# Attention with beacon keys, then a squared-ReLU MLP: last 128 output rows as two column halves, scores in 14 pieces per batch, attention released at four head pairs per MLP chunk

## The chip, the cores and the metric

The kernel runs on one core of one Trainium2 chip. The metric is the time of one execution on the device in microseconds (us); the kernel before takes 343.65 us, the median of 3 runs (343.54 to 343.87). Engines are named as in the profile: PE (matmul), PEld (the load of a matmul's stationary operand), ACT, DVE, POOL and SP. SP computes nothing here, it issues DMAs.

## The reference

All inputs and the output are float32. Attention has B=8 batches, H=8 heads, S=576 tokens and D=64, with Nb=16 beacon keys in front of each batch's keys that every token may see. The output of attention, laid out as 4608 tokens by 512, goes through an MLP whose middle is the square of a ReLU.

```python
k_all = np.concatenate([beacon_k, k], axis=2)           # 592 keys
v_all = np.concatenate([beacon_v, v], axis=2)
scores = scale * np.matmul(q, k_all.transpose(0, 1, 3, 2))
causal[:, Nb:] = np.triu(np.ones((S, S), dtype=bool), k=1)
scores = np.where(causal, -1000000000.0, scores)
a = np.exp(scores - scores.max(-1, keepdims=True))
a /= a.sum(-1, keepdims=True) + 1e-09
x = np.matmul(a, v_all).transpose(0, 2, 1, 3).reshape(B * S, H * D)
h = x @ w_in                                            # 512 -> 2048
out = np.square(np.maximum(h, 0.0)) @ w_out             # 2048 -> 512
```

## The kernel before

**Attention** goes by head pairs: 4 pairs per batch, 32 in all, numbered p. Keys of a batch are cut into 5 tiles c (four of 128 and one of 80). A score matmul (line 753) has a key tile as its stationary operand and a range of query columns t0 to t1 as its moving one; the two heads of a pair lie on the two halves of the PE's rows, so each entry of a piece is two matmuls. Only columns that the causal mask leaves are computed. A **piece** is what one exponential on ACT (line 768) takes: up to 512 columns in each of two neighbouring PSUM banks (one bank per head), written as bf16 into the tile `pt`. The list `WHOLE` (line 681) cuts a pair into 4 pieces of 496, 464, 416 and 288 columns, 1664 in all, from 6 key-tile ranges, so 12 matmuls. Batch 0 uses another list, `SPLIT`. Then come the mask on DVE (lines 783 and 787), 30 matmuls of probabilities by values (line 803, with a column of ones that gives the sums), and the division on DVE (lines 818 and 819) into `xn`. For batches 1 to 7 a DMA transpose (line 850, five per batch, issued by SP) brings `xn` to `xT`, which the MLP reads.

**The MLP** goes by 9 chunks of 512 tokens: 64 matmuls of 512 columns with w_in (line 931), ReLU on ACT or DVE (lines 948 and 950), the square on DVE (line 957), 64 matmuls of 512 columns with w_out (line 968: 4 blocks of 128 tokens, 16 matmuls each), an ACT copy of each block into `osb` (line 437), and a store to `out` (line 991; for the last 256 rows one store per block, line 993). Chunk j needs tokens 512j to 512j+511; so chunks 3 to 7 each need a first part of the batch of the same number.

**Loads**: q and k of batches 3 to 7 come as float32 through 8 staging tiles `stg` (lines 483 and 484 on SP), are cast on POOL (line 439) into `qk_area`, and are transposed by two DMAs per batch (line 516 on SP) into `qT` and `kT`. There are two buffers of each, so batch b writes where batch b-2 was read.

**The order of the work** is fixed when the program is built. Every step is an `Op` with an engine, an assumed duration and a priority; `Order.run` (line 154) plays them against pools of PSUM banks, staging and `pt` tiles and a model of the DMA queues, and writes each engine's instructions out in the order that results. On the chip each engine runs its list in that order, with semaphore waits. What matters here:

- Score pieces are taken in groups, several pieces with 2 banks each at once: `SIZES` (line 705) gives [3, 3, 3, 3, 2, 2] for the 16 pieces of the 4 pairs of a batch from 2 on, and eight groups of 2 for batch 1. A group is one run of matmuls on PE.
- `gate` (line 717) lets pair p >= 4 start only when the MLP work done on PE has reached 27.7 us times (LEAD + PACE (p - 4)); `PACE` is 0.225 (line 711).
- SP takes loads, both kinds of transposes and stores in one list, and an instruction that waits holds all behind it.

```python
WHOLE = [Phase(
    pieces=[
        ([(0, 0, 496, 0)], 0, 496),                       # (key tile, t0, t1, column), offset in pt, width
        ([(1, 112, 576, 0)], 512, 464),
        ([(2, 240, 576, 0), (0, 496, 576, 336)], 1024, 416),
        ([(3, 368, 576, 0), (4, 496, 576, 208)], 1536, 288),
    ],
SIZES = {b: [2] * 8 if b < 2 else [3, 3, 3, 3, 2, 2] for b in range(B)}
LEAD, PACE = -0.4, 0.225
```

Of the kernel before, what the change touches and what calls it, by code (L numbers as in the profile page):

```python
# [310 lines left out]
def kernel(  # L311
# [11 lines left out]
    nc = tc.nc  # L323
# [17 lines left out]
    def sb(name, shape, dt):  # L341
        return pool.tile(shape, dt, name=name)
# [24 lines left out]
    pt = [sb(f"pt{i}", [128, 2, 2048], BF16) for i in range(NPT)]  # L367
# [7 lines left out]
    tri = sb("tri", [128, 4, 128], BF16)  # L375
# [46 lines left out]
    def emit_tri(e):  # L422
        for i in range(4):
            nc.gpsimd.affine_select(out=tri[:, i, :], in_=tri[:, i, :], compare_op=ALU.is_ge, fill=0.0,
                                    base=Nb if i == 0 else 0, pattern=[[1, 128]], channel_multiplier=-1)
# [26 lines left out]
    def t_start(t):  # L452
        return max(0, 128 * t - Nb)
# [222 lines left out]
    whole_off = {}  # L676
    for t in range(NT):
        for c in range(t + 1):
            whole_off[c, t] = ((t_start(t) if t < 4 else 1360) if c == 0 else
                               1744 if c == 4 else 512 * c + 128 * (t - c))  # L680
# [23 lines left out]
    SIZES = {b: [2] * 8 if b < 2 else [3, 3, 3, 3, 2, 2] for b in range(B)}  # L704
# [5 lines left out]
    LEAD, PACE = -0.4, 0.225  # L710
# [23 lines left out]
    def add_scores(pairs, n, sizes):  # L734

        work = [(x, i, piece) for x in pairs for i, piece in enumerate(phases(x.b)[n].pieces)]
        exps = {x.p: [] for x in pairs}
        at = 0
        for size in sizes:
            group = work[at:at + size]  # L740
            at += size
            prio = 100.0 * group[0][0].p + 1000.0 * n + group[0][1]
            cols = sum(t1 - t0 for _, _, (mms, _, _) in group for _, t0, t1, _ in mms)
            owners = list({x.p: x for x, _, _ in group}.values())
            box = {}

            def emit_qk(e, group=group, box=box):
                for k, (x, _, (mms, _, _)) in enumerate(group):
                    st = pair(box["qk"], k)
                    for c, t0, t1, col in mms:  # L750
                        for hj in range(2):
                            hp = slice(64 * hj, 64 * hj + 64)
                            nc.tensor.matmul(  # L753
                                st[:, hj, col:col + t1 - t0],
                                kT[x.b % 2][hp, x.pr, 128 * c:128 * c + 128],
                                qT[x.b % 2][hp, x.pr, t0:t1],
                                start=True, stop=True,
                            )

            qk = add(f"qk{group[0][0].p}.{n}.{group[0][1]}", "PE", cols / 2400.0, emit_qk, prio=prio,  # L760
                     deps=[d for x in owners for d in x.qk_deps + [x.take_pt]],
                     take=("ps", "late" if b < NSPLIT and n else "strip", [2] * size), gate=owners[0].gate, mode="rows")
# [3 lines left out]
            for k, (x, i, (_, off, width)) in enumerate(group):  # L766
                def emit_exp(e, off=off, width=width, k=k, x=x, box=box):
                    nc.scalar.activation(pt[x.take_pt.held[0]][:, :, off:off + width],  # L768
                                         pair(box["qk"], k)[:, :, 0:width], AF.Exp, bias=0.0, scale=scale)

                exps[x.p].append(add(f"exp{x.p}.{n}.{i}", "ACT", act(2 * width), emit_exp, prio=prio + 0.1 * k,
                                     deps=[qk], give=(qk, k)))
# [133 lines left out]
    def add_chunk(j):  # L906
# [11 lines left out]
        for f in range(NFT // 2):  # L918
            sqs = []
            for n, (lo_, hi_) in enumerate(parts):  # L920
# [34 lines left out]
                def emit_sq(e, f=f, lo=lo_ - t0, hi=hi_ - t0):  # L955
# [7 lines left out]
                  [(ts, f0) for ts in range(4) for f0 in range(0, NFT, step)])  # L963
        for n, (ts, f0) in enumerate(order2):
# [12 lines left out]
            s2_ops[j, ts] = o  # L977
        for u in range(2):
            evs = []
            for ts in (2 * u, 2 * u + 1):  # L980
# [14 lines left out]
            if j == NCH - 1 and u == 1:  # L995
                st_ops[2 * j + u] = [add(f"st{j}.{u}.{ts}", "SP", 0.65,
                                         lambda e, emit_st=emit_st, ts=ts: emit_st(e, ts=ts),
                                         prio=-20.0, deps=[evs[ts]], dma=0.7, packet=0.092) for ts in range(2)]
            else:
                st_ops[2 * j + u] = [add(f"st{j}.{u}", "SP", 0.65, emit_st, prio=-20.0, deps=evs, dma=1.4, packet=0.092)]  # L1000
# [7 lines left out]
    for b in range(B):  # L1008
# [26 lines left out]
        if b < NSPLIT:  # L1035
            for x in pairs:
                for n, ph in enumerate(phases(b)):
                    add_scores([x], n, [1] * len(ph.pieces))
        else:
            add_scores(pairs, 0, SIZES[b])  # L1040
# [48 lines left out]
```

## Time and profile before

| What | us |
|---|---|
| median of 3 runs | 343.65 |
| the profiled execution, its own time | 344.22 |
| its span (first to last instruction) | 342.4 |
| PE busy, ACT busy, DVE busy in the span | 325.1, 195.0, 160.3 |

The profiled execution took 0.57 us more than the median of the unprofiled runs, and 1.8 us of it lie outside the span. The granted PE clock was 1.0 of full speed in the whole span. How to read the rows: a group is "line engine operation output<-input, shape, xcount | busy us, mean ns of one | idle time before, and what ended it". A row of the chain of waits or of the timeline begins with the start and the length in us. "SPq" is SP's list of DMA issues. A matmul's row includes the way of its last column through the array, so the means of matmuls (379 ns for 512 columns) overlap; their rate is read from runs of many.

### The profile page before, as it was taken

How to read it: one execution, taken by the hardware profiler on the slowest of the kernel's cores; microseconds unless marked ns; L12 is line 12 of the kernel's file. 1: busy time of each engine (PE TensorE's matmuls, PEld its weight loads, DVE VectorE, ACT ScalarE, POOL GpSimd, SP SyncE). 2: the span in 40 equal slices, each digit the busy share in tenths (PEclk: the TensorE clock that was granted, in tenths of full speed). 3: DMA queues.
4: the chain of work that ended last, by engine and by line, in shares of the span. 5: the costliest groups of instructions: out<-in, count | busy, mean ns of one | idle time of the engine just before them, and what ended most of it. 6: DMA issues, size and time to landing. Idle time of an engine off the chain costs nothing.

```text
span 342.4 us, 7074 instructions
## 1 busy us (share of the span) xinstructions
PE 325.1 (95%) x2838; PEld 175.7 (51%) x2876; DVE 160.3 (47%) x323; ACT 195.0 (57%) x301; POOL 81.1 (24%) x129
## 2 busy tenths in 40 slices
PE   2999999999999999999999799999999999999995
PEld 2677665454544544453557574444544444444442
DVE  6788978177425842385524483287403202301400
ACT  3987873588358564577554754597326326515611
POOL 6545802516124222423241126020000000000000
PEclk9999999999999999999999999999999999999999
DMA  9999999699979996999999889980041011011002
GB/s 166 197 205 221 206 204 208 134 252 204 188 164 215 197 199 145 255 188 224 133 209 220 184 177 207 219 170 24 15 117 63 0 61 63 0 61 63 0 29 93
DMA packets 139472, 50.33 MB, mean 147 GB/s; under 512 B 125808, under 2 KB 134512, under 8 KB 139440
## 3 DMA queue, kind: packets, MB, share of 16 engines
q1 hardware_dynamic: 129856, 40.91, 58.1%
q0 software_dynamic: 9376, 8.69, 15.5%
q8 instruction: 22, 0.36, 0.5%
q10 hardware_dynamic: 208, 0.29, 0.3%
q14 instruction: 10, 0.08, 0.1%
HBM read 37.22 MB, written 9.44 MB: 136 GB/s over the span
## 4 chain that ended last, share of the span: by engine, by line
PE 66%; DMA 19%; SPq 7%; DVE 4%; issue 2%; POOL 2%; ACT 1%; POOLq 0%; DVEq 0%; ACTq 0%
PE ps L931 28%; PE ps L968 26%; PE ps L803 5%; SPq L850 5%; PE ps L753 5%; DMA kT<-qk_area 5%; DMA stg<-in_k_dram 4%; DMA bks<-in_beacon_k_dram 3%; DMA stg<-in_v_dram 3%; DVE g L957 2%; DMA stg<-in_q_dram 1%; DMA qk_area<-in_q_dram 1%; SPq L484 1%; POOL w_in L892 1%; PE ps L635 1%
## 5 line engine op out<-in xcount | busy, mean ns | idle before, releaser
L931 PE MATMUL ps<-xT,w_in 128*128 128x512 bf16 (+3 forms) x688 | 134.3, 340 | 1.1 <-DMA xT<-xn 0.2
L968 PE MATMUL ps<-w_out,g 128*128 128x512 bf16 x554 | 127.9, 379 | 1.1 <-issue 0.2
L768 ACT ACTIVATE pt<-ps 128x832 bf16<-128x832 f32 (+4 forms) x128 | 102.9, 872 | 28.6 <-PE ps L753 28.5
L931 PEld LDWEIGHTS <-w_in 128*128 128x128 bf16 x704 | 64.9, 98 | 57.8 <-issue 7.7
L957 DVE TENSOR_TENSOR g<-g 128x1024 bf16<-128x1024 bf16 (+2 forms) x80 | 53.6, 673 | 76.9 <-ACT g L948 75.6
L948 ACT ACTIVATE g<-ps 128x512 bf16<-128x512 f32 (+2 forms) x117 | 66.3, 567 | 39.9 <-PE ps L931 39.2
L968 PEld LDWEIGHTS <-g 128*128 128x128 bf16 x576 | 54.1, 98 | 64.1 <-issue 2.9
L437 ACT COPY osb<-ps 128x512 f32<-128x512 f32 x36 | 21.3, 591 | 65.0 <-PE ps L968 60.4
L439 POOL CAST vb<-stg 128x512 bf16<-128x512 f32 (+1 forms) x36 | 24.3, 684 | 84.3 <-DMA stg<-in_v_dram 39.9
L439 POOL CAST qk_area<-stg 128x512 bf16<-128x512 f32 (+2 forms) x50 | 32.1, 645 | 50.6 <-DMA stg<-in_q_dram 33.8
L783 DVE TENSOR_TENSOR pt<-pt,tri 128x1024 bf16<-128x1024 bf16 (+1 forms) x36 | 23.9, 667 | 31.3 <-ACT pt L768 31.3
L803 PEld LDWEIGHTS <-pt 128*128 128x128 bf16 (+1 forms) x960 | 33.6, 98 | 7.6 <-issue 1.2
L950 DVE TENSOR_SCALAR g<-ps 128x512 bf16<-128x512 f32 (+2 forms) x43 | 25.7, 600 | 24.9 <-PE ps L931 24.5
L803 PE MATMUL ps<-vb,pt 128*128 128x65 bf16 (+1 forms) x960 | 34.9, 194 | 1.3 <-DVE pt L783 0.5
L753 PE MATMUL ps<-qT,kT 64*128 64x80 bf16 (+7 forms) x400 | 33.5, 282 | 2.6 <-DMA kT<-qk_area 2.1
L819 DVE TENSOR_TENSOR xn<-ps,rcp 128x640 bf16<-128x640 f32 (+2 forms) x36 | 27.0, 750 | 1.5 <-DVE rcp L818 0.2
L753 PEld LDWEIGHTS <-kT 64*128 64x128 bf16 x400 | 13.5, 96 | 23.2 <-issue 15.4
L818 DVE RECIPROCAL rcp<-ps 128x10 f32<-128x10 f32 (+2 forms) x36 | 7.5, 208 | 23.1 <-PE ps L803 23.0
L437 ACT COPY qT<-ps 128x576 bf16<-128x576 bf16 x12 | 7.5, 640 | 6.4 <-PE ps L635 5.0
L439 DVE COPY kT<-ps 128x576 bf16<-128x576 bf16 x12 | 8.9, 751 | 2.8 <-PE ps L638 1.9
L787 DVE TENSOR_TENSOR pt<-pt,tri 80x160 bf16<-80x160 bf16 x32 | 10.0, 312 | 0.0
L635 PE MATMUL ps<-ident,sparek 96*128 96x96 bf16 x18 | 1.5, 229 | 6.0 <-DVE sparek L439 6.0
(49 smaller groups left out, 71.7 us busy)
## 6 DMA issues: line engine op xcount, KB each, us to landing
out_dram<-osb SPq DMA_DIRECT2D x17, 512.0 KB, 3.3
stg<-in_v_dram SPq DMA_DIRECT2D x21, 256.0 KB, 5.0
stg<-in_q_dram SPq DMA_DIRECT2D x20, 256.0 KB, 4.7
stg<-in_k_dram SPq DMA_DIRECT2D x15, 256.0 KB, 5.1
w_in<-in_moe_w_in_dram POOLq DMA_DIRECT2D x4, 512.0 KB, 8.2
w_out<-in_moe_w_out_dram POOLq DMA_DIRECT2D x4, 512.0 KB, 10.9
stg<-in_v_dram SPq DMA_DIRECT2D x7, 224.0 KB, 4.2
qk_area<-in_k_dram POOLq DMA_DIRECT2D x4, 288.0 KB, 12.7
```

Of the source, the lines that this page charges most:

```text
L437: nc.scalar.copy(dst, src)
L439: eng[e].tensor_copy(dst, src)
L753: nc.tensor.matmul(st[:, hj, col:col + t1 - t0], kT[x.b % 2][hp, x.pr, 128 * c:128 * c + 128], qT[x.b % 2][hp, x.pr, t0:t1], start=True, s ...
L768: nc.scalar.activation(pt[x.take_pt.held[0]][:, :, off:off + width], pair(box["qk"], k)[:, :, 0:width], AF.Exp, bias=0.0, scale=scale)
L783: nc.vector.tensor_tensor(out=d, in0=d, in1=tri[:, m0:m0 + m, :][:, None].to_broadcast([128, 2, m, 128]), op=ALU.min)
L803: nc.tensor.matmul(a[:, hj, (t - tl[0]) * (D + 1):(t - tl[0] + 1) * (D + 1)], P[0:rr, hj, o:o + 128], vb[b % 2][0:rr, c, h, :], start=(c = ...
L819: nc.vector.tensor_tensor(out=xn[b % 2].rearrange("p t (h d) -> p h t d", d=D)[:, 2 * pr:2 * pr + 2, tl[0]:tl[0] + nt], in0=a[:, :, :, 0:D ...
L931: nc.tensor.matmul(h[:, lo - spans[0][0]:hi - spans[0][0]], w_in_sb[:, mc, ft * 128:(ft + 1) * 128], xT[:, mc, lo % RING:lo % RING + hi - lo],
L948: nc.scalar.activation(dst, h, AF.Relu, bias=0.0, scale=1.0)
L950: nc.vector.tensor_scalar(out=dst, in0=h, scalar1=0.0, scalar2=None, op0=ALU.max)
L957: nc.vector.tensor_tensor(out=d, in0=d, in1=d, op=ALU.mult)
L968: nc.tensor.matmul(o, G[:, fc, ts * 128:(ts + 1) * 128], w_out_sb[:, fc, :], start=(fc == 0), stop=(fc == NFT - 1))
```

## The change

1. **The last 128 rows** of the last chunk are computed by `add_closing` as two halves of 256 output columns, 16 matmuls of 256 columns each. The first half is copied by ACT and stored by SP. The second is copied in two quarters, one by ACT and one by DVE; ACT issues the store of its quarter itself, SP that of DVE's. The other block of these 256 rows keeps a store of its own.
2. **The pieces**: a pair has 1664 columns as before, now as 512 + 512 + 512 + 128, from 11 ranges (22 matmuls), five of them of 80 columns. From batch 2 on the pieces of 128 columns of two pairs share one pair of banks, so that 4 pairs make 14 bank pairs, in groups of [3, 3, 3, 3, 2]. Batch 1 keeps groups of two pieces. There are 4 exponentials per pair as before. The offsets in `pt`, the mask's stride and a fifth triangle in `tri` follow from that.
3. **The gate**: `PACE` is 0.25 instead of 0.225.

```diff
-            for lo, hi in ((928, 1024), (1440, 1536), (1824, 2048)):
+            for lo, hi in ((928, 1024), (1440, 1536), (1824, 2000)):
...
-        for i in range(4):
+        for i in range(5):
...
     WHOLE = [Phase(
         pieces=[
-            ([(0, 0, 496, 0)], 0, 496),
-            ([(1, 112, 576, 0)], 512, 464),
-            ([(2, 240, 576, 0), (0, 496, 576, 336)], 1024, 416),
-            ([(3, 368, 576, 0), (4, 496, 576, 208)], 1536, 288),
+            ([(0, 0, 112, 0)] + [(c, 496, 576, 112 + 80 * c) for c in range(NT)], 1152, 512),
+            ([(1, 112, 496, 0), (3, 368, 496, 384)], 0, 512),
+            ([(0, 112, 368, 0), (2, 240, 496, 256)], 512, 512),
+            ([(0, 368, 496, 0)], 1024, 128),
         ],
-        diag=(0, 512, 0, 4), last=1744, tiles=range(NT), off=whole_off)]
+        diag=(0, 384, 1, 4), last=1584, tiles=range(NT),
...
-    SIZES = {b: [2] * 8 if b < 2 else [3, 3, 3, 3, 2, 2] for b in range(B)}
+
+    ONE_BY_ONE = [[(x, i)] for x in range(HP) for i in range(4)]
+    SHARED = [[(0, 0)], [(0, 1)], [(0, 2)], [(0, 3), (1, 3)], [(1, 0)], [(1, 1)], [(1, 2)], [(2, 0)], [(2, 1)],
+              [(2, 2)], [(2, 3), (3, 3)], [(3, 0)], [(3, 1)], [(3, 2)]]
+    PIECES = {b: ONE_BY_ONE if b < 2 else SHARED for b in range(B)}
+    SIZES = {b: [2] * 8 if b < 2 else [3, 3, 3, 3, 2] for b in range(B)}
...
-    LEAD, PACE = -0.4, 0.225
+    LEAD, PACE = -0.4, 0.25
...
+        closing = j == NCH - 1
+        if closing:
+            order2 = [x for x in order2 if x[0] < 3]
...
+        if closing:
+            add_closing(j, base + 120, G, sq)
         for u in range(2):
             evs = []
-            for ts in (2 * u, 2 * u + 1):
+            for ts in ((2,) if closing and u else (2 * u, 2 * u + 1)):
...
+    def add_closing(j, prio, G, sq):
+
+        d, rows = osb[(2 * j + 1) % 2], slice(j * TCH + 384, j * TCH + 512)
+        half = d_model // 2
+        before = st_ops[2 * j - 1]
+        for c in range(2):
+            s2 = []
+
+            def emit_s2(e, c=c, s2=s2):
+                for f in range(NFT):
+                    nc.tensor.matmul(bank(s2[0])[:, 0:half], G[:, f, 384:512], w_out_sb[:, f, c * half:(c + 1) * half],
+                                     start=(f == 0), stop=(f == NFT - 1))
+
+            s2.append(add(f"s2.{j}.3.{c}", "PE", MM * NFT / 2, emit_s2, prio=prio + c,
...
+                          take=("ps", "mlp", [1]), pe_time=MM * NFT / 2))
+            parts = [("ACT", 0, half)] if c == 0 else [("ACT", 0, half // 2), ("DVE", half // 2, half)]
+            outs = []
+            for by, lo, hi in parts:
+                at = slice(c * half + lo, c * half + hi)
+
+                def emit_ev(e, lo=lo, hi=hi, at=at, s2=s2):
+                    copy_on(e, d[:, 1, at], bank(s2[0])[:, lo:hi])
+
+                ev = add(f"ev{j}.3.{c}.{by}", by, act(hi - lo), emit_ev, prio=-15.0, deps=s2 + before)
+                outs.append(ev)
+                queue = "ACT" if c and by == "ACT" else "SP"
+
+                def emit_st(e, at=at):
+                    (nc.scalar if e == "ACT" else nc.sync).dma_start(out=out[rows, at], in_=d[:, 1, at])
+
+                add(f"st{j}.3.{c}.{by}", queue, 0.65, emit_st, prio=-20.0, deps=[ev], dma=0.7 * (hi - lo) / d_model,
+                    packet=0.05)
+            add(f"done{j}.{c}", "-", 0.0, None, deps=outs, give=s2[0])
```

More of the change, by code (lines that the diff above doesn't have):

```diff
@@ L366 @@
     kT = [sb(f"kT{i}", [128, HP, NT * 128], BF16) for i in range(2)]
[L367 removed]
+    pt = [sb(f"pt{i}", [128, 2, 2000], BF16) for i in range(NPT)]
     xn = [sb(f"xn{i}", [128, NT, H * D], BF16) for i in range(2)]
@@ L745, in add_scores @@
+            owners = list({x.p: x for x, _, _, _ in every}.values())
             box = {}
             def emit_qk(e, group=group, box=box):
-                for k, (x, _, (mms, _, _)) in enumerate(group):
+                for k, parts in enumerate(group):
                     st = pair(box["qk"], k)
[L750 to L758, printed above, removed]
@@ L761, in add_scores @@
+            qk = add(f"qk{lead.p}.{n}.{group[0][0][1]}", "PE", cols / 2400.0, emit_qk, prio=prio,
                      deps=[d for x in owners for d in x.qk_deps + [x.take_pt]],
-                     take=("ps", "late" if b < NSPLIT and n else "strip", [2] * size), gate=owners[0].gate, mode="rows")
+                     take=("ps", "late" if lead.b < NSPLIT and n else "strip", [2] * size), gate=lead.gate, mode="rows")
             box["qk"] = qk
@@ L993, in emit_st @@
                     nc.sync.dma_start(out=out[t0 + 128 * ts:t0 + 128 * ts + 128, :], in_=d[:, ts, :])
[L995 to L1000, printed above, removed]
+            last = closing and u
```

63 lines of the change are left out of this document (42 added, 21 removed).

## The prediction

> **What bounds the kernel now.** I read the page's shares first, then the windows, then what PE waited for, then the chain at the one long wait.
>
> ```profile
> span 342.4 us, 7074 instructions
> PE 325.1 (95%) x2838; PEld 175.7 (51%) x2876; DVE 160.3 (47%) x323; ACT 195.0 (57%) x301; POOL 81.1 (24%) x129
> PE   2999999999999999999999799999999999999995
> DMA  9999999699979996999999889980041011011002
> ```
>
> PE is busy in 95% of the span and below nine tenths only in the first, the last and one slice in between (slice 23, 188 to 197 us). ACT and DVE are half idle. The DMA engines are nearly full for 27 slices, to about 230 us, and then nearly idle: the loads and transposes are squeezed into the time in which attention runs.
>
> ```profile
> 162.00:196.00 34.00, 31.77 (x325) 20.29 (x324) 13.93 (x25) 19.69 (x29) 8.68 (x15) 1.00 1.05 190
> 196.00:230.00 34.00, 33.78 (x314) 18.00 (x316) 18.50 (x32) 20.58 (x32) 10.18 (x16) 1.00 0.98 187
> ```
>
> The second and third numbers are the length and PE's busy time: 2.2 us are missing in the first window, 0.2 in the second. The waits name them (total, times, longest):
>
> ```profile
> PE ps L753 <- DMA kT<-qk_area: 2.1, 1, 2.1
> PE ps L803 <- DVE pt L783: 0.5, 1, 0.5
> PE ps L803 <- DVE xn L819: 0.5, 1, 0.5
> PE ps L753 <- ACT pt L768: 0.4, 1, 0.4
> PE ps L931 <- DMA xT<-xn: 0.2, 1, 0.2
> ```
>
> and the chain shows what came ahead of the long one:
>
> ```profile
> 175.52 4.98 DMA stg<-in_v_dram
> ...
> 181.91 0.53 SPq L991
> ...
> 182.54 7.74 DMA kT<-qk_area
> ...
> 190.32 0.76 PE ps L753 x8
> ```
>
> The first scores of batch 6 wait 2.1 us for the key transpose of their batch, which SP issued at 182.54 us, behind a value load and a store. So the kernel is PE's instruction list, plus a few waits, plus a tail. A change helps if it shortens that list, removes one of these waits, or shortens what follows PE's last matmul.
>
> **1. The gate (PACE 0.25).** It removes no instruction; it puts MLP matmuls ahead of the scores. Counting in the built order of PE: ahead of the first scores of batch 5 stand 428 MLP matmuls of 512 columns before and 464 after; of batch 6, 540 and 592; of batch 7, 644 and 720. One costs 0.216 us (45 in 9.71):
>
> ```profile
> 324.63 9.71 PE ps L968 x45
> ```
>
> So batch 6 needs its keys 52 x 0.216 = 11.2 us later, batch 5 7.8 us and batch 7 16.4 us later. The wait goes unless the key transpose comes later by more than 11.2 - 2.1 = 9.1 us. In SP's new list it is moved behind the five xT transposes of batch 4, the query transpose, the rest of the loads and the store of the second half of chunk 3. That store is the last to come free: chunk 3's w_out matmuls end 76 MLP matmuls (16.4 us, and attention beside them) ahead of the first scores of batch 6, while an ACT copy (0.59), the store's issue (0.53) and the transpose (7.74) take 8.9. About 7 us are left. I take the whole 2.1 us off; bounds 0 to 2.4 (a 0.2 us wait of batch 5 with it).
>
> What is late next is xT. From the last probabilities-by-values run of a batch to the w_in matmuls that read it, the new order leaves 48 MLP matmuls (10.4 us; for batch 5 64) and, but for batch 7, 3.4 us of attention; before it left 84 or more for the same batches from 4 on.
>
> ```profile
> L819 DVE TENSOR_TENSOR xn<-ps,rcp 128x640 bf16<-128x640 f32 x28 | 23.1, 824 | 1.1
> L818 DVE RECIPROCAL rcp<-ps 128x10 f32<-128x10 f32 x28 | 6.1, 216 | 22.8 <-PE ps L803 22.7
> 189.80 6.72 SPq L850 DMA_TRANSPOSE xT<-xn  x5
> 65.70 2.48 DMA xT<-xn
> ```
>
> The path is 0.22 + 0.82 on DVE, three of SP's five issues (3 x 1.34 = 4.0) and a landing of 2.5: 7.5 us of 13.8, so SP may be 6 us late. It is moved behind nine loads of the batch after next. I cost it at nothing; without that cover it is the second rival.
>
> **2. The pieces.** The columns stay 1664 per pair. Exponentials stay four per pair:
>
> ```profile
> L768 ACT ACTIVATE pt<-ps 128x832 bf16<-128x832 f32 x36 | 31.2, 873 | 15.4 <-PE ps L753 15.3
> L768 ACT ACTIVATE pt<-ps 128x928 bf16<-128x928 f32 x32 | 30.5, 954 | 2.8 <-PE ps L753 2.8
> L768 ACT ACTIVATE pt<-ps 128x992 bf16<-128x992 f32 x28 | 28.1, 1003 | 7.5 <-PE ps L753 7.5
> L768 ACT ACTIVATE pt<-ps 128x576 bf16<-128x576 f32 x28 | 18.4, 658 | 2.9 <-PE ps L753 2.9
> ```
>
> By their slope, (1003 - 658) / 416 = 0.83 ns per column, 1024 columns take 1.03 us and 256 take 0.39: 3 x 1.03 + 0.39 = 3.48, against 3.49 before. Nothing on ACT. On PE a change between scores and other matmuls costs time on both sides:
>
> ```profile
> 50.46 0.91 PE ps L803 x30
> ...
> 53.20 0.41 PE ps L753 x8
> 53.61 1.83 PE ps L968 x8
> ...
> 101.56 1.73 PE ps L968 x8
> ...
> 206.30 0.62 PE ps L753 x10
> ```
>
> Eight w_out matmuls take 1.83 us behind scores and 1.73 behind probabilities by values: 0.10. The run of ten has 1200 columns per head, 0.51 us at 0.216 per 512, and takes 0.62: 0.10 more and 0.01 for its five pairs. The new order has 50 score runs on PE for 56, so 6 x 0.20 = 1.2 us less. Against it stand 280 more score matmuls (680 for 400), 140 pairs of heads: at 0.002 to 0.0055 per pair 0.3 to 0.8 us; I take 0.7, as runs of five 80-column pairs are not in the trace. **Sum -0.5 us.** The lower end is -0.9. The upper end comes from the values' rows: 30 matmuls with a weight load each take 0.91, so 30 ns each with 27 ns of columns; if two heads' short matmuls could not go together at less than that, it would be +4.7 (third rival).
>
> The Trainium skill, "TensorE: Matmul & The Clock Gate", section "Back-to-back issue gap", speaks against short matmuls: in streams of a load and a matmul it gives some 81 ns for each of 128 columns. By that, as an estimate, the 280 added matmuls would cost 11 us more even with the heads two at a time (280 x 0.081 / 2). This trace does not bear it out, with 30 ns for 65 columns.
>
> Fewer, fuller bank pairs also change when a values' run may start. The shortest way in the new order is 2.4 us (a score run of 0.75 and 8 MLP matmuls) from the start of a score group to the values' run that needs its first piece: 0.21 to the first result (0.05 of columns, and the 0.16 by which the row of a 512-column matmul exceeds 0.216), 0.39 for the exponential, and the mask.
>
> ```profile
> L968 PE MATMUL ps<-w_out,g 128*128 128x512 bf16 x554 | 127.9, 379 | 1.1 <-issue 0.2
> L783 DVE TENSOR_TENSOR pt<-pt,tri 128x1024 bf16<-128x1024 bf16 x28 | 20.7, 739 | 31.3 <-ACT pt L768 31.3
> L787 DVE TENSOR_TENSOR pt<-pt,tri 80x160 bf16<-80x160 bf16 x32 | 10.0, 312 | 0.0
> ```
>
> With 0.74 + 0.31 and three semaphore steps of about 0.05 (the chain above leaves 0.10 for two, from 182.44 to 182.54) that is 1.8 us: 0.6 to spare, and about as much where the first piece has 1024 columns and the way is 3.4 us; ten places in all. A DVE instruction of 0.7 us in the way eats that. The waits for DVE above (0.5 and 0.5) show that it happens; I add **+0.4 us**, bounds 0 to 3. The fifth triangle is one more POOL instruction at 5.6 us:
>
> ```profile
> 5.61 1.49 POOL L424 TENSOR_SCALAR_AFFINE_SELECT tri<-tri 128x128 bf16<-128x128 bf16 x4
> 11.86 0.61 POOL L439 CAST vb<-stg 128x512 bf16<-128x512 f32 x1 [4.75 <-DMA stg<-in_v_dram]
> ```
>
> 1.49 / 4 = 0.37 us in 4.75 us of idle time: nothing. The shorter pads cost nothing either.
>
> **3. The last rows.**
>
> ```profile
> 337.41 2.09 SPq L993 DMA_DIRECT2D out_dram<-osb  x2
> 338.54 0.59 ACT L437 COPY osb<-ps 128x512 f32<-128x512 f32 x1 [1.15 <-PE ps L968]
> out_dram<-osb SPq DMA_DIRECT2D x1, 512.0 KB, 2.8
> out_dram<-osb SPq DMA_DIRECT2D x2, 256.0 KB, 2.0
> L437 ACT COPY xT<-ps 128x240 bf16<-128x240 bf16 x1 | 0.4, 358 | 0.0
> L439 DVE COPY xT<-ps 128x240 bf16<-128x240 bf16 x3 | 0.8, 276 | 0.0
> ```
>
> Now: copy 0.59, then the store, 2.0 us from issue to landing, then the program's end. After: PE's end comes about 0.05 later (16 more matmuls and a shorter last one). A quarter of 128 columns takes 0.26 on ACT (0.59 and 0.36 at 512 and 240 columns). The **two engines do not run side by side**: in the built instructions DVE's copy waits for ACT's count to reach the value that the very copy of the other quarter sets, and not for PE. So it is 0.26, a semaphore step of 0.05 and DVE's copy, 0.14 to 0.28 by its row, taken as 0.2: 0.51 for 0.59. The two stores are of 64 KB; from 512 to 256 KB the landing shrank by 0.8, so 64 KB would land in 1.4 by size alone, and in 2.0 if rows of 512 bytes go no faster than rows of 2 KB; I take 1.6. The ACT queue hides ACT's own store behind DVE's copy. The stores ahead have the 1.7 us of the last half block's matmuls to get away. Sum 0.05 - 0.08 - 0.4 = **-0.4 us**; bounds -0.75 to +0.2.
>
> The Trainium skill, "PSUM — Partial Sum Buffer", section "Terms", states that two engines at one bank and quadrant at once collide, reads against reads too. Both quarters lie in one bank, which is why the copies are put one behind the other; on two banks the tail would be some 0.2 us shorter.
>
> **The sum** against the profiled execution: span 342.4 - 2.3 (key waits) - 0.5 + 0.4 - 0.4 = 339.6; with the 1.8 us outside the span (344.22 - 342.4) 341.4, and less 0.57, by which that execution exceeded the median (343.65), 340.8. I say **341.0 us**, 0.8% faster; own range 339.4 to 342.4.
>
> **Rivals.**
> - *The wait moves along* (0.10). The DMA engines are full, the gate only spreads the demand, and the key transposes, now behind later stores on SP, come as late as they are needed. For it: 1.05 of DMA share in the window of the wait. Against it: DMA is idle after 230 us, and the new order needs the last batches 16 us later. Then -2.3 falls away: 343.2.
> - *xT comes late* (0.07). If SP reaches the xT transposes more than 6 us behind the division, each of batches 2, 3, 4 and 6 waits on PE. At 0.5 us each 343.0, at 1.0 us 345.0; I put it at 343.5.
> - *Short score matmuls are bound by their weight loads* (0.11; the other side). If PE can't take a load and a matmul faster than one per 30 ns, a pair's five 80-column entries take 10 x 30.5 = 305 ns for 167 of columns, and its 112- and 128-column ones some 30 ns more: 0.17 us x 28 pairs = 4.7 us, so 345.7, slower. It decides above some 0.10 us per pair. Against it: the run of ten above has four such short matmuls and took only 0.62, where this would make it 0.67; but there long ones stand between.
> - *The forecast* (0.72).
>
> 0.2%, 0.7 us, is about what a measurement of this kernel can tell from no change. Faster by more: the forecast, 0.04 of the first rival and 0.03 of the second, 0.79. Within it: 0.09. Slower: the third rival and the worst of the second, 0.12. The range of 8 in 10 reaches from the forecast's low end over the first two rivals: 339.4 to 343.6.
>
> **What would show it.** PE's wait for kT is gone, and its busy share in 162 to 196 us is that of the neighbours; DMA stays busy some 20 us longer. Score runs of twenty matmuls take about 0.75 us (1536 columns: 0.65 + 0.10); over 0.85 speaks for the third rival. PE's waits for DVE stay below 1.5 us in total, those for xT below 0.5. At the end DVE's copy starts after ACT's ends, and from PE's last matmul to the span's end it is about 0.4 us shorter. I am wrong if PE shows a wait of over 1 us for xT or kT, or if the early part, up to 20 us, changes.

## The result, and the profile after

The changed kernel took **339.99 us** (median of 4 executions, 339.65 to 340.3) against 343.76 us (343.54 to 344.7) for the kernel before, timed beside it: a ratio of 0.9892 with an interval from 0.9863 to 0.9922. The prediction was 341.0. A second group of runs, of the ninth to twelfth experiments below, gave 340.16 against 344.06 us, a ratio of 0.9874 (0.984 to 0.9908). Comparisons leave disturbed executions out; the one profile in this study that fell into such an execution, that of the fifth experiment, is read for its order and its clock and not for its span.

The page of the profile after: span, busy time, and two rows of the 40 slices.

```profile
span 338.1 us, 7659 instructions
PE 323.5 (96%) x3134; PEld 183.0 (54%) x3172; DVE 161.8 (48%) x325; ACT 194.5 (58%) x301; POOL 81.8 (24%) x130
PE   3989999999999999999999999999999999999995
DMA  9999999889988999799989999892310041011003
```

The span is 4.3 us shorter. PE's slice at seven tenths, 188 to 197 us, is gone. The slice at eight tenths, 17 to 25 us, is new; the wait for w_in named below lies in it. DMA falls off at slice 28, as before, though not all at once. The windows (start and end, length, PE's busy time with its count, then PEld, DVE, ACT and POOL, the granted clock, the DMA share, GB/s), of after and then of before for the third window:

```profile
162.00:196.00 34.00, 33.68 (x391) 23.67 (x393) 16.01 (x29) 21.49 (x32) 10.28 (x16) 1.00 0.99 188
196.00:230.00 34.00, 33.78 (x302) 17.05 (x305) 16.23 (x27) 21.07 (x31) 10.56 (x16) 1.00 1.08 194
230.00:254.00 24.00, 23.68 (x251) 12.62 (x254) 7.92 (x15) 13.48 (x22) 0.00 (x0) 1.00 0.24 70
```

```profile
230.00:254.00 24.00, 23.79 (x225) 12.69 (x227) 10.50 (x21) 11.19 (x18) 0.00 (x0) 1.00 0.19 50
```

In 162 to 196 us PE now misses 0.3 us where it missed 2.2. Behind 230 us the DMA share went from 0.19 to 0.24. SP's last key transpose, in the timeline of after, is issued at 222.83 us:

```profile
222.83 4.69 SPq L516 DMA_TRANSPOSE kT<-qk_area  x1
```

In before it was 215.66 (below): 7 us later, not the 20 that the prediction had said for DMA. What PE waited for in the kernel after (total, times, longest):

```profile
PE ps L635 <- DVE sparek L439: 5.6, 1, 5.6
PE ps L947 <- DMA w_in<-in_moe_w_in_dram: 1.0, 1, 1.0
...
PE ps L947 <- DVE g L966: 0.7, 1, 0.7
PE ps L764 <- ACT pt L781: 0.5, 1, 0.5
PE ps L819 <- DVE rcp L834: 0.4, 1, 0.4
```

Neither kT nor xT is among them. The first row is the start, which both kernels have; the wait for w_in is at 18 us, that for `g` at 38 us. The prediction had named a change of the part up to 20 us as a sign of being wrong. The wait for w_in is such a change by the letter, but not one that the new program brings each time: the second profile of the same kernel has no wait for w_in, and the old kernel with only the new end has 0.5 us of it. What became of the score runs stands in the chain of waits:

```profile
170.89 1.73 PE ps L987 x8
...
198.56 0.77 PE ps L764 x20
...
204.62 0.67 PE ps L764 x20
205.28 1.83 PE ps L987 x8
```

In the chain a run of twenty score matmuls takes 0.77 us (1536 columns per head) or 0.67 (1280), about the 0.75 that was forecast and under the 0.85 that would have spoken for the weight loads. Eight w_out matmuls take 1.83 us behind scores and 1.73 elsewhere, as before.

**Where the time went, in three parts.** The traces offer two marks. One is the first ACT copy of an MLP result (the first of the rows below); ahead of it stand, in both kernels, the same columns of scores (those of batches 0 and 1) and of probabilities by values. The other is the 32nd such copy, behind which only the last chunk is left, 64 matmuls with w_in and the last with w_out. First before, then after:

```profile
63.63 0.58 ACT L437 COPY osb<-ps 128x512 f32<-128x512 f32 x1 [1.95 <-PE ps L968]
...
310.89 0.58 ACT L437 COPY osb<-ps 128x512 f32<-128x512 f32 x1 [1.15 <-PE ps L968]
```

```profile
64.37 0.59 ACT L437 COPY osb<-ps 128x512 f32<-128x512 f32 x1 [1.95 <-PE ps L987]
...
307.16 0.59 ACT L437 COPY osb<-ps 128x512 f32<-128x512 f32 x1 [1.15 <-PE ps L987]
```

The start went from 63.63 to 64.37 (+0.74 us), the middle from 247.26 to 242.79 (-4.47), the end (342.4 - 310.89 and 338.1 - 307.16) from 31.51 to 30.94 (-0.57). The same marks are used for every experiment. They are worth it: three profiled executions with the new pieces and the steeper gate (two of the changed kernel, and the ninth experiment) have the middle at 242.79 us each, while their starts are 64.37, 63.41 and 65.31. Four more, which differ from them only in the last rows, have 242.82 to 243.29. **With the steeper gate an execution differs from the next mostly in its first 65 us.** Without it this does not hold, as the fifth experiment shows.

### The profile page after: what moved, and what is told of

It is laid out like the page before. It is cut to its first block, busy times and chain, and to the rows that moved or that the text cites. A ratio compares the mean times of both kernels' runs of the same rounds, so it can differ in the third digit from the quotient of the medians.

```text
span 338.1 us, 7659 instructions
## 1 busy us (share of the span) xinstructions
PE 323.5 (96%) x3134; PEld 183.0 (54%) x3172; DVE 161.8 (48%) x325; ACT 194.5 (58%) x301; POOL 81.8 (24%) x130
## 4 chain that ended last, share of the span: by engine, by line
PE 89%; DMA 5%; DVE 2%; issue 2%; ACT 1%; SPq 0%; POOL 0%; ACTq 0%; POOLq 0%
PE ps L947 36%; PE ps L987 35%; PE ps L819 8%; PE ps L764 7%; DMA w_in<-in_moe_w_in_dram 2%; DMA stg<-in_v_dram 1%; DMA qk_area<-in_q_dram 1%; PE ps L1030 1%; PE ps L635 1%; ACT pt L781 1%; DVE g L966 1%; DVE g L973 0%; DVE kT L439 0%; ACT osb L437 0%; DVE xn L835 0%
## 5 line engine op out<-in xcount | busy, mean ns | idle before, releaser
L987 PE MATMUL ps<-w_out,g 128*128 128x512 bf16 x536 | 125.4, 379 | 1.8 <-issue 0.8
L781 ACT ACTIVATE pt<-ps 128x1024 bf16<-128x1024 f32 (+3 forms) x128 | 102.3, 871 | 18.2 <-PE ps L764 18.0
L987 PEld LDWEIGHTS <-g 128*128 128x128 bf16 x560 | 51.9, 98 | 60.7 <-issue 3.9
L437 ACT COPY osb<-ps 128x512 f32<-128x512 f32 (+2 forms) x37 | 21.3, 576 | 71.3 <-PE ps L987 55.7
L439 POOL CAST qk_area<-stg 128x512 bf16<-128x512 f32 (+2 forms) x50 | 33.4, 674 | 69.4 <-DMA stg<-in_k_dram 41.9
L439 POOL CAST vb<-stg 128x512 bf16<-128x512 f32 (+1 forms) x36 | 23.4, 661 | 64.3 <-DMA stg<-in_v_dram 35.7
L966 DVE TENSOR_SCALAR g<-ps 128x512 bf16<-128x512 f32 (+2 forms) x44 | 26.8, 610 | 19.5 <-PE ps L947 19.4
L764 PE MATMUL ps<-qT,kT 64*128 64x80 bf16 (+6 forms) x680 | 33.1, 234 | 0.5 <-ACT pt L781 0.5
L764 PEld LDWEIGHTS <-kT 64*128 64x128 bf16 x680 | 18.9, 96 | 17.2 <-issue 14.6
```

The lines of the kernel that those rows point to most:

```text
L437: nc.scalar.copy(dst, src)
L439: eng[e].tensor_copy(dst, src)
L764: nc.tensor.matmul(st[:, hj, lo + col:lo + col + t1 - t0], kT[x.b % 2][hp, x.pr, 128 * c:128 * c + 128], qT[x.b % 2][hp, x.pr, t0:t1], sta ...
L966: nc.vector.tensor_scalar(out=dst, in0=h, scalar1=0.0, scalar2=None, op0=ALU.max)
L987: nc.tensor.matmul(o, G[:, fc, ts * 128:(ts + 1) * 128], w_out_sb[:, fc, :], start=(fc == 0), stop=(fc == NFT - 1))
```

## The experiments

The theory: the gate takes the wait for kT away and gives nearly all of the gain. The rivals: the pieces do (fewer score runs); the gate gains by some other effect of a new order; the end does. The first four runs were made on one chip (the kernel before there: 344.22 us).

### The gate alone

```diff
-    LEAD, PACE = -0.4, 0.225
+    LEAD, PACE = -0.4, 0.25
```

> The kernel before with PACE 0.25 alone. Theory (the gate takes PE's wait for the key transpose of batch 6 away, and little else): 2.2 to 3.0 us faster than before, ratio about 0.992; no wait of PE for kT; 592 MLP matmuls of 512 columns ahead of batch 6's first scores as in the changed kernel. Rival 'pieces' (fewer and fuller score groups did it): under 0.7 us faster, the kT wait still there or another in its place.

Measured: 340.75 us, ratio 0.991 (0.9881 to 0.994), so by the ratio 3.1 us faster, just over the expected range. Among PE's waits there is no kT, and one for xT. The marks:

```profile
PE ps L931 <- DMA xT<-xn: 0.5, 1, 0.5
```

```profile
65.05 0.58 ACT L437 COPY osb<-ps 128x512 f32<-128x512 f32 x1 [1.96 <-PE ps L968]
...
309.22 0.58 ACT L437 COPY osb<-ps 128x512 f32<-128x512 f32 x1 [1.15 <-PE ps L968]
```

The middle is 244.17 us, 3.09 shorter than before. That is more than the 2.1 us of the kT wait (2.2 by the starts of the matmuls). Listing PE's gaps from the starts of its matmuls, a gap of 0.64 us ahead of the values' run at 111.9 us is gone too. That run waited for DVE's division of the run ahead of it (line 819, 111.89 to 112.71 us in before); in the new order the division is over at 111.5 and the next run starts at 116.7, behind more MLP matmuls. The two are 2.8 us. Against them stand 0.3 us more of wait for xT, so some 0.5 of the 3.1 us are not accounted for.

### The pieces alone

All of the new pieces, banks and groups, with `PACE` at 0.225 and the old end:

```diff
+    PIECES = {b: ONE_BY_ONE if b < 2 else SHARED for b in range(B)}
+    SIZES = {b: [2] * 8 if b < 2 else [3, 3, 3, 3, 2] for b in range(B)}
...
     LEAD, PACE = -0.4, 0.225
```

> The kernel before with the new pieces and groups alone, PACE 0.225 and the old tail. Theory: batch 6's first scores stand behind 540 MLP matmuls as before, so the kT wait of about 2 us stays; 6 fewer score runs on PE at 0.2 us less about 0.45 for 140 more pairs of matmuls: 0.5 to 0.9 us faster, ratio about 0.998. Rival 'pieces': 2.5 us faster or more.

Measured: 349.05 us, ratio 1.0145 (1.0113 to 1.0177): by the ratio 5.0 us **slower**, a miss for every theory stated. The waits show a new one, for value tiles:

```profile
PE ps L819 <- POOL vb L439: 4.8, 3, 3.4
PE ps L819 <- DVE pt L799: 0.6, 1, 0.6
...
PE ps L764 <- DMA kT<-qk_area: 0.4, 1, 0.4
```

The wait for kT fell to 0.4 us by itself. SP's issues in the timeline say why the values are late. First with the pieces alone, then before (its first row is the key transpose spoken of above):

```profile
219.76 0.57 SPq L484 DMA_DIRECT2D stg<-in_v_dram  x1
220.42 6.44 SPq L866 DMA_TRANSPOSE xT<-xn  x5
226.96 1.30 SPq L1012 DMA_DIRECT2D out_dram<-osb  x1
228.31 1.78 SPq L484 DMA_DIRECT2D stg<-in_v_dram  x2
```

```profile
215.66 3.00 SPq L516 DMA_TRANSPOSE kT<-qk_area  x1
...
219.34 3.21 SPq L484 DMA_DIRECT2D stg<-in_v_dram  x3
222.65 6.43 SPq L850 DMA_TRANSPOSE xT<-xn  x5
```

No load was touched by the edit. But the groups take PSUM banks and `pt` tiles in another rhythm, presumably this shifts the planner's times, and in the order that results two of the last three value loads of batch 7 end up behind five transposes and a store. They are issued at 228.31 instead of some 220 us, and PE starts no matmul from 229.9 to 233.5, which is the 3.4 us of the list and the time of the last matmul itself. (The third wait, 1.0 us, ends at 135.6 us; the fifth experiment still has waits there.) And PE does not come back at once. The windows around it:

```profile
230.00:234.00 4.00, 0.34 (x6) 0.21 (x5) 0.47 (x1) 1.08 (x2) 1.10 (x2) 1.00 0.67 145
234.00:238.00 4.00, 3.82 (x24) 1.68 (x23) 1.66 (x3) 0.60 (x1) 0.13 (x1) 0.57 0.00 0
238.00:242.00 4.00, 4.00 (x35) 1.92 (x35) 2.07 (x6) 3.56 (x5) 0.00 (x0) 1.00 0.00 0
```

In the four microseconds from 234 us the granted clock is 0.57, and 512-column matmuls follow each other at 427 ns instead of 216. That costs (1 - 0.57) x 4 = 1.7 us more. All six executions show it (mean clock 0.995 of the span). The sum of the middle, against before: value waits +4.8, clock +1.7, kT -1.7, the values' wait at 111.9 us -0.6, and the pieces' own saving (-0.9, below) make +3.3; measured are 250.65 - 247.26 = +3.4.

### The end alone

The whole of part 1 of the change, with the old pieces and `PACE` at 0.225:

```diff
+        if closing:
+            add_closing(j, base + 120, G, sq)
```

> The kernel before with the new last rows alone. Theory: 0.4 to 0.6 us faster (ratio about 0.9985), all behind PE's last matmul, with DVE's copy starting after ACT's; the body as before with its kT wait. If the copies ran side by side 0.8 us.

Measured: 344.05 us, ratio 1.0008 (0.9978 to 1.0038); the interval is wider than the effect. The traces decide: from the 32nd copy to the end of the span 30.96 us, against 31.51 before. The other traces of the old end have 31.48 (the gate alone), 31.42 (the later gate) and 31.50 (the ninth experiment); the others of the new end have 30.94, 31.0 and 31.03. So the end is worth **0.5 us**, and no more hangs on it.

### One gate, later

Only batches 6 and 7 are released later; the order of all that comes earlier stays that of before. 564 MLP matmuls stand ahead of the first scores of batch 6, where it was 540, and 592 in the changed kernel.

```diff
-            return o.progress >= mlp_chunk_us * (LEAD + PACE * (p - HP))
+            return o.progress >= mlp_chunk_us * (LEAD + PACE * (p - HP) + (0.3 if b >= 6 else 0.0))
```

> The kernel before with PACE 0.225, and only the pairs of batches 6 and 7 let in 0.3 chunk later: 564 MLP matmuls ahead of batch 6's first scores in place of 540, that is 5.2 us later; all before that in the same order. Theory (one wait, a matter of when its scores are asked for): the wait of 2.1 us is gone, 1.9 to 2.3 us faster, ratio about 0.994. Rival 'spread' (the gain of the gate comes from a lighter DMA load over all batches, and a local delay only moves the wait to the next transpose): under 0.7 us faster, with a wait for kT or xT of 1 us or more at batch 6 or 7.

Measured: 341.61 us, ratio 0.9935 (0.9905 to 0.9965), so 2.2 us faster; PE shows no wait for kT. The middle is 308.18 - 63.66 = 244.52 us, 2.74 shorter. A shift of 24 matmuls (24 x 0.216 = 5.2 us) at a single place brings most of what the gate brings, and the rival of a general effect falls. (0.3 of the 2.74 us are a shorter wait for the division at 112 us, where the edit changes nothing.)

### The pieces alone, values first

The kernel of the second experiment, with the five transposes of batch 6 put behind the last value load of batch 7 in SP's list. PE's list is unchanged.

```diff
+    for t in range(NT):
+        named[f"xt6.{t}"].behind = [named["ld7v4"]]
     with tc.manual_schedule():
```

> e2_pieces with one change of SP's list and none of PE's: the last two value loads of batch 7 stand ahead of the five xT transposes of batch 6 and a store, not behind them. Theory (in e2_pieces PE lost its time to value casts that came late because their loads stood behind a store that waited for ACT): the waits for POOL's casts at 230 and 234 us, 4.2 us by the trace, fall under 1 us, and the kernel is 3.3 to 4.2 us faster than e2_pieces, ratio to before 1.001 to 1.005. Rival (the DMA engines are full, a wait only moves; or the new score groups themselves cost it): it stays over 1.010, with another wait of 3 us or more on PE.

Measured: 343.97 us, ratio 0.9961 (0.9919 to 1.0002), with the kernel before at 345.13 us on this chip. Against 1.0145 that is 1.8% less, some 6 us; the expected 3.3 to 4.2 us are short of that. The 1.7 us of clock that go with the pause, which I had not counted, would fill most of the gap. The lists of PE, ACT, DVE and POOL are those of the second experiment, so the order on SP is what made the pieces slow.

The trace can't show where the six microseconds went, because the profiled execution was the longest of the ten (347.93 us; the shortest took 341.21). Its middle is 250.45 us, no shorter than the 250.65 of the second experiment. The waits for vb at 230 and 234 us are gone from it, but it waits 3.9 us in three for kT. One of these waits, 1.7 us at 190.7 us, lies ahead of the place that the edit touches, and the second experiment's profile has none there: in the same order the key transpose was issued at 185.71 us in the one execution and at 181.28 in the other. So without the steeper gate the middle too differs from one execution to the next, and the waits for kT are not put down to the edit. Behind the one that ends at 225.6 us, 1.9 us long, the clock falls again:

```profile
223.00:226.00 3.00, 1.06 (x18) 0.44 (x17) 0.99 (x2) 1.03 (x2) 0.00 (x0) 1.00 0.91 174
226.00:230.00 4.00, 3.78 (x18) 1.46 (x15) 0.89 (x2) 2.86 (x3) 1.19 (x3) 0.58 1.13 209
230.00:232.00 2.00, 2.00 (x26) 0.99 (x26) 1.19 (x2) 0.87 (x2) 0.60 (x2) 0.99 0.49 99
```

### Three other ends

Each is the changed kernel with another end, and was run once. In the first ACT alone copies the second half, and SP stores it in one piece:

```diff
-            parts = [("ACT", 0, half)] if c == 0 else [("ACT", 0, half // 2), ("DVE", half // 2, half)]
+            parts = [("ACT", 0, half)]
...
-                queue = "ACT" if c and by == "ACT" else "SP"
+                queue = "SP"
```

> The changed kernel with the second half of 256 columns copied by ACT alone and stored by SP as one store. Theory (the split copies run one behind the other, 0.27 + 0.02 + 0.29 us): the copy is 0.37 us and SP issues 0.2 us earlier; the store is twice as large; from PE's last matmul to the span's end 0 to 0.2 us shorter than in the changed kernel. If the split had saved time, 0.1 us or more longer.

In the second the two column parts are 384 and 128 wide, each copied by ACT and stored by SP:

```diff
+        wide, base_ = (384, 128), (0, 384)
...
-            parts = [("ACT", 0, half)] if c == 0 else [("ACT", 0, half // 2), ("DVE", half // 2, half)]
+            parts = [("ACT", 0, wide[c])]
```

> The changed kernel with the last 128 rows cut into 384 and 128 columns, each copied by ACT alone and stored by SP. Theory: behind PE's last matmul stands one copy of 0.27 us and one store of 64 KB, so the tail is 0.3 us shorter than in the changed kernel; PE's sixteen matmuls of 128 columns take 0.9 us. Rival: the store of 384 columns, issued late, now ends last, or the short matmuls are bound by their weight loads, and nothing is gained.

In the third the two quarters are computed into two PSUM banks, with 32 matmuls of 128 columns, so that DVE's copy waits for PE and not for ACT:

```diff
+                n = half // (c + 1)
                 for f in range(NFT):
-                    nc.tensor.matmul(bank(s2[0])[:, 0:half], G[:, f, 384:512], w_out_sb[:, f, c * half:(c + 1) * half],
+                    for i in range(c + 1):
+                        nc.tensor.matmul(bank(s2[0], i)[:, 0:n], G[:, f, 384:512],
+                                         w_out_sb[:, f, c * half + i * n:c * half + (i + 1) * n],
```

> The changed kernel with the two quarters of the second half in two PSUM banks, 32 matmuls of 128 columns. Theory (one bank is what puts the copies one behind the other): DVE's copy starts within 0.1 us of ACT's and not 0.29 later; SP's last issue comes 0.2 to 0.3 us sooner after PE's last matmul; PE itself 0.05 us later. Rival: DVE starts late anyway.

Measured: 339.94, 340.15 and 338.92 us, with spans of 338.2, 338.5 and 337.1. From the 32nd copy to the end of the span they take 30.85, 30.91 and 31.0 us, the changed kernel 30.94. The last rows of the timeline, for the changed kernel, for ACT alone, and for two banks:

```profile
332.85 1.91 PE L1030 MATMUL ps<-w_out,g 128*128 128x256 bf16 x16
...
334.80 0.27 ACT L437 COPY osb<-ps 128x128 f32<-128x128 f32 x1 [1.16 <-PE ps L1030]
335.09 0.37 ACTq L1049 DMA_DIRECT2D out_dram<-osb  x1
335.09 0.29 DVE L439 COPY osb<-ps 128x128 f32<-128x128 f32 x1 [12.83 <-ACT osb L437]
335.41 0.33 SPq L1049 DMA_DIRECT2D out_dram<-osb  x1
```

```profile
334.99 0.37 ACT L437 COPY osb<-ps 128x256 f32<-128x256 f32 x1 [1.16 <-PE ps L1030]
335.38 0.33 SPq L1049 DMA_DIRECT2D out_dram<-osb  x1
```

```profile
333.72 0.27 ACT L437 COPY osb<-ps 128x128 f32<-128x128 f32 x1 [1.15 <-PE ps L1032]
333.78 0.29 DVE L439 COPY osb<-ps 128x128 f32<-128x128 f32 x1 [12.57 <-PE ps L1032]
334.01 0.39 ACTq L1052 DMA_DIRECT2D out_dram<-osb  x1
334.10 0.33 SPq L1052 DMA_DIRECT2D out_dram<-osb  x1
```

In the changed kernel DVE starts at 335.09, when ACT's 0.27 us are over: the two quarters take 0.61 us to the last issue, and one copy of 256 columns by ACT alone takes 0.39. The second engine and the second queue bring nothing. With two banks the copies do run side by side, and the last store is issued 0.38 us after the first copy's start instead of 0.61; but from there to the end it is 337.1 - 334.10 = 3.0 us instead of 338.1 - 335.41 = 2.69, and the gain is gone. The rows of the issues (KB of one, median us from issue to landing), for the changed kernel and for two banks, have part of that:

```profile
out_dram<-osb SPq DMA_DIRECT2D x1, 64.0 KB, 1.7
```

```profile
out_dram<-osb SPq DMA_DIRECT2D x1, 64.0 KB, 1.9
```

Two stores issued 0.09 us apart land 0.2 later each than two issued 0.32 apart. That is the whole of it: taken to two decimals from the traces, SP's store lands 1.93 us behind its issue instead of 1.69, and the span ends 1.05 us behind that landing in both. Why the stores land later was not settled. The narrow end missed its expectation, 0.3 us shorter, in a like way: its last store is issued 0.29 us behind the start of the copy and 0.57 behind the store of the other block, and from there to the end it is 2.94 us.

What all these ends share is that the last block goes out in two column parts, and with ACT alone two halves are enough. Where the change saves is seen beside before: there it took 0.61 us as well from the start of the last copy to the last issue (338.54 to 339.15), so nothing is gained up to the issue. The last store lands after 1.69 us instead of 2.04, and from the landing to the end of the span it is 1.05 us instead of 1.17. The shorter span of the third end lies in its start (63.09 us to the first copy), not in its end.

### What is left: gate and pieces, gate and end, and the change again

Four kernels on one more chip (the kernel before there: 344.06 us). The changed kernel with the old end:

```diff
-        closing = j == NCH - 1
+        closing = False
```

> The changed kernel with the old end of the last 128 rows, that is, the kernel before with the steeper gate and the new score pieces. Theory (in the traces the pieces save 0.66 us of entries into score runs and cost 0.45 us of extra head-pair matmuls, so that with the steeper gate they are worth about 0.2 us, and what they cost alone is the value loads behind the transposes): no TensorE wait for kT, none over 1 us on the values; the tail from TensorE's last matmul to the end of the span 0.4 to 0.6 us longer than the changed kernel's; span 338 to 339.5 us, ratio to the kernel before 0.988 to 0.992. Rival (the pieces spoil the value loads with the steeper gate too): a wait on vb over 1 us, span over 340.5, ratio over 0.994.

The kernel before with the steeper gate and the new end, and the old pieces:

```diff
-    LEAD, PACE = -0.4, 0.225
+    LEAD, PACE = -0.4, 0.25
...
+        if closing:
+            add_closing(j, base + 120, G, sq)
```

> The kernel before with the steeper gate and the new end, but the old score pieces. Theory (pieces worth about 0.2 us): within 0.8 us of the changed kernel, span 337.8 to 339.2, ratio to the kernel before 0.987 to 0.991, 48 score runs after 20 us entered at 0.096 us each. Rival (the pieces are worth as much as the difference of 2.6 us between the changed kernel's span and that of the gate alone, less 0.5 for the end): span over 339.8 and a ratio 0.005 above that of the changed kernel on the same chip.

The changed kernel with no edit:

> The changed kernel itself, unaltered, as the measure for the other three on the same chip. Span 337 to 339 us, ratio 0.987 to 0.991; the waits before 40 us (w_in, the beacon keys, the first down projection) come out anywhere from 0 to 2 us in sum.

And the end in two banks once more (the diff as above), now run more often:

> The same kernel as the one-look run with the last two quarters in two banks, now timed. Theory (its span was 1.0 us shorter through waits before 40 us that differ from one execution to the next; its tail from the last matmul on was no shorter, since the stores landed later by what the copy gained): within 0.2% of the changed kernel on the same chip. Rival (the copies side by side save 0.3 us and more): ratio 0.002 or more below the changed kernel's.

| Kernel | us | ratio to before, interval | to first copy | middle | end |
|---|---|---|---|---|---|
| gate and pieces | 340.31 | 0.9889 (0.9857 to 0.9922) | 65.31 | 242.79 | 31.50 |
| gate and end | 340.82 | 0.9914 (0.9882 to 0.9947) | 64.60 | 243.67 | 31.03 |
| the change again | 340.16 | 0.9874 (0.984 to 0.9908) | 63.41 | 242.79 | 31.00 |
| end in two banks | 340.54 | 0.9893 (0.9857 to 0.9928) | 64.61 | 243.29 | 31.00 |

The marks of the second row:

```profile
64.60 0.59 ACT L437 COPY osb<-ps 128x512 f32<-128x512 f32 x1 [1.95 <-PE ps L971]
...
308.27 0.59 ACT L437 COPY osb<-ps 128x512 f32<-128x512 f32 x1 [1.15 <-PE ps L971]
```

The times alone can't part the four: their intervals overlap. The middles can. With the steeper gate, old pieces take 243.67 (and 244.17 in the first experiment, which has 0.5 us of xT wait in it), new ones 242.79: **the pieces are worth about 0.9 us once the gate is there**. Against the longest of the seven middles with new pieces, 243.29, it would be 0.4. The expectation of 0.2 us was too low, and its rival too high: in the middle there are 36 score runs with the old pieces and 30 with the new, 6 x 0.20 = 1.2 us less, and the added pairs of heads cost 0.3 to 0.4. Values come in time in both kernels with gate and pieces: no wait on vb. The ninth run shows a wait of 1.2 us of a w_in matmul for DVE's ReLU; it ends at 40.3 us, in the start. One thing more can be read from these ends. In the narrow one and in the two banks the matmuls of 128 columns start 56 ns apart, in the narrow one with a weight load for each: not the 81 ns that the prediction quoted against short matmuls. The end in two banks is not faster, as expected, and no version of these is measurably faster than the change itself.

## Why the prediction was right

- **The gate, forecast -2.3: right in its mechanism, too small.** The kT wait went, as the gate alone and the single late gate show. In the profiled executions the middle gave 3.1 us in the gate alone and 3.6 with the new end beside it, where PE has no wait for xT. Of what goes beyond the 2.3, 0.64 us is what a values' run waited for the division at 111.9 us. The prediction saw that wait (0.5 in its rows), but as a sign of what the pieces would make worse, not as one that the gate would take away. The wait is no fixed size either: 2.1 us in the profile of before, 1.6 in that of the end alone.
- **The 7 us to spare for the key transpose: less, and by another way.** In the kernel after, it lands at 196.0 us and the scores start at 198.5, 2.5 us to spare; in the second profile of that kernel it is 6.6. The prediction took the store ahead of it for the last to come free. Its last copy was over at 179.4 us, but SP issued it at 186.83, behind four value loads on which it spent 5.2 us. That the margin held was partly luck.
- **xT, forecast nothing: right.** No wait for xT in the kernel after; 0.5 us once in the gate alone, at 69 us, where before has 0.2.
- **DMA busy 20 us longer: wrong**, without harm. The scores of batch 7 start 13.0 us later in the traces (220.7 and 233.7 us; the 16.4 us of matmuls, less what was saved until then), its key transpose was issued only 7 us later, and the share behind 230 us rose by 0.05.
- **The pieces, forecast -0.5: right in sign and mechanism** with the gate, -0.9. The switch of 0.20 us per run held; the added pairs cost 0.3 to 0.4 instead of the 0.7 taken. The third rival fell: twenty-matmul runs take 0.67 to 0.77 us.
- **Waits of values' runs, forecast +0.4: the step that failed.** In the middle they went down: the 0.5 us for a division at 111.9 us in before is in none of the nine profiles with the steeper gate. The margin of 0.6 us was reckoned for the shortest way from scores to values, and its ten places did not come up short. The waits at 13 and 41 us, for a division and a mask, lie in the start and are no measure: in the fourteen profiles the one at 41 us is anything from nothing to 0.9 us, with old pieces and new.
- **What the prediction did not see**: that the pieces move two value loads behind transposes. It said of the pieces only what they do on PE and took their order from the kernel with all parts. Alone they cost 5.0 us. Nothing in its working says that the value loads would come in time with the gate; that they do is luck as far as the prediction goes. The change as a whole was right for a reason that stands in its third part.
- **The end, forecast -0.4: right**, -0.5. DVE's copy does start after ACT's, as forecast. The two cost 0.61 us to the last issue, as the one copy did in before, so the 0.08 us that the prediction gave them came to nothing. A store of 64 KB lands in 1.7 us for the 1.6 taken, and 0.1 us more is saved behind the landing. The prediction's remark that two banks would save some 0.2 us more was wrong: 31.0 against 30.94. The Trainium skill, "PSUM — Partial Sum Buffer", section "Terms", states that two engines at one bank and quadrant at once collide. No run here shows a collision, since within one bank the program itself orders the copies.
- **The sum.** Forecast for the profiled execution: -2.8 us. Middle and end of the traces give -4.5 and -0.6, the start +0.7. Whether the start is really longer is open: to the first copy it took 63.1 to 64.2 us in the five kernels with `PACE` 0.225 and 63.1 to 65.3 in the nine profiles with 0.25, on three chips. The medians, -3.8 and -3.9, lie between the two sums.

## What to carry to other kernels

Judge a change to a planned order by the whole list of every engine and queue that results, not by the engine that it is meant for: here an edit of PE's work alone put two loads behind a row of transposes, and only another part of the change made that harmless. Find two marks in the trace between which the work is the same in all versions. Where PE waits for no DMA between them, single profiles of one program agreed within 0.5 us there, where five rounds of timing left intervals of 0.3% (1 us) each way. And count a long pause of PE at more than its length, since it can cost clock as well.

## What the runs showed of the hardware that was not expected

**A pause of PE can cost its clock.** Behind a pause of 3.4 us (pieces alone) and one of 1.9 us (values first, with 0.7 us of short score matmuls behind it) PE ran for about 3.4 us at half rate, 427 ns for 512 columns, and lost 1.7 us each time. All six executions of the pieces alone have it, of the ten with values first only the profiled one. In the profile of before the pause of 2.1 us cost no clock: 1.00 in the windows around it. But 7 of the 32 executions of before on the first two chips of the experiments have a mean clock of 0.995, which is 0.005 x 343 = 1.7 us; none of the 13 on the third has. So part of what the gate saves may be this clock in some executions; that was not measured by itself. The Trainium skill, "TensorE: Matmul & The Clock Gate", section "HAM oscillation — how this bites in real kernels", gives as a rule no idle gaps of PE over some 3.4 us, and the section "What's actually happening" has half rate last one window of 3.4 us that runs free of the kernel. The length of the half rate agrees with these traces, 3.4 us in both; the one case of 1.9 us shows that a pause well below 3.4 us can be enough.

**With the steeper gate the scatter is in the start; without it, in the DMA too.** Seven profiles with the same program up to the last rows took 63.09 to 65.31 us to the first copy; their middles lie between 242.79 and 243.29. That does not mean that the DMAs keep time: in the two profiles of the changed kernel the key transpose of batch 6 was issued at 187.87 and 185.23 us and landed at 196.0 and 190.95. PE only has enough work ahead of the scores not to notice.
